# Where the last two copies of attention weights stand among ScalarE's work

## The chip, the core and the metric

The kernel runs on one core of a Trainium2 chip. The core has five engines with a queue each: TensorE (PE in the profile, with its weight loads as PEld), VectorE (DVE), ScalarE (ACT), GpSimd (POOL) and SyncE (SP, which here issues all DMAs). They run side by side and wait for each other by semaphores. The metric is the time of one execution on the device in microseconds (us); less is better. A profile is one further execution, recorded by the hardware profiler, with a time of its own.

## What is computed

Attention in which each query keeps only its 32 largest scores, followed by a two-layer network over all tokens. Batch 8, 8 heads, 576 positions, 64 per head, so 4608 tokens of 512 values; the hidden layer has 2048.

```python
scores = scale * np.matmul(q, k.transpose(0, 1, 3, 2))
kth = np.partition(scores, -top_k, axis=-1)[..., -top_k:-top_k + 1]
scores = np.where(scores >= kth, scores, -1000000000.0)
attn = np.exp(scores - np.max(scores, axis=-1, keepdims=True))
attn = attn / (np.sum(attn, axis=-1, keepdims=True) + 1e-09)
x = np.matmul(attn, v)          # then heads side by side: (4608, 512)
h = x @ w_in
g = np.where(h >= 1, h, np.where(h <= -1, 0.0, (h + 1) ** 2 / 4))
out = g @ w_out
```

All of it is in float32.

## The kernel before

**Steps.** The attention is cut into 144 steps (`n = 144`, `m` from 0 to 143). A step takes 128 queries of two heads. VectorE finds the 32nd largest score of each query, ScalarE takes the exponential, VectorE masks it (L467) and sums it. Four steps fill one chunk of 128 tokens; a chunk then goes through the network. There are 36 chunks, and the last is filled by the steps 140 to 143.

**From weights to values.** When step `m` begins, `divide` of step `m - 1` is issued: VectorE's reciprocal (L413), and on GpSimd the scaling of both heads' weights (L420) and a small subtraction into `excess` (L423). For step 143 there is no following step, so its `divide` comes in its own last slot. The weights must then be transposed for TensorE. In all but the first steps this goes by DMA: `move_w` (L493) has ScalarE split the float32 words into two halves of 16 bits (L497, two copies, one for each head, into the tile `halves`), writes them to DRAM (`rows<-halves`, L499), and puts the transposing read (`wT<-rows`, recorded at L296) on a list. The list `reads_of_rows` is issued by L832, in slot 0 of a step, and from step 141 on in every slot. `halves` has one buffer, `rows` three, `wT` four. `values` (L506) multiplies `wT` with the values (L514) into a PSUM buffer `po`, which ScalarE copies to `xT` (L527).

**The network.** `hidden(x)` is one piece of the first layer: sixteen matmuls (L547) for 256 of the 2048 hidden values of a chunk, so pieces 0 to 7. ScalarE reads a piece twice from PSUM, into `r` (L558) and `g` (L566), here called its reading. GpSimd then bounds, squares and adds (L573, L575, L576). `r` has two buffers: the reading of piece x waits until GpSimd is through with piece x - 2. `final(f)` is a matmul of the second layer (L586). Pieces and `po` share three PSUM buffers. The last chunk works in pieces of 128 and in half rows of the output (L561 to L563, L600, L612), with VectorE in GpSimd's place.

**Order.** The kernel writes out the order on each engine by hand (`tc.manual_schedule`). Each step has 7 slots. In each slot the top-k work goes first, then the transposes, then the copies of the weights, then the values, and last `advance` takes network work from the list `pending` up to an allowance. The closing steps 144 and 145 have no top-k work. Around the end, ScalarE's order is this. Step 143: reading 2 (slot 0), reading 3 (slot 1), reading 4 (slot 2), copy of step 142's weights (slot 3), reading 5 (slot 5). Step 144: `xT` copies of steps 140 and 141 (slot 2), copy of step 143's weights (slot 3). Step 145: readings 6 and 7, `xT` copies of 142 and 143, then the last chunk. TensorE in the same stretch: pieces 1 to 4, finals 0 and 1, piece 5, finals 2 and 3, values 140 and 141, piece 6, finals 4 and 5, piece 7, finals 6 to 9, values 142 and 143, the transpose `pworst`, finals 10 and 11, and then the last chunk's pieces between the remaining finals. GpSimd: piece 0, scaling and `excess` of 142, pieces 1 to 4, scaling and `excess` of 143, pieces 5 to 7.

The lines that place a copy:

```python
if slot == 3 and 1 <= m <= n and state[m - 1] is not None and not state[m - 1]["by_tensor"]:
    move_w(state[m - 1])
    ready_at[m - 1] = done[m - 1] + 15.0
```

`ready_at` is an estimate for the planner; its value for a step doesn't depend on the slot.

Of the kernel before, what the change touches and what calls it, by code (L numbers as in the profile page):

```python
# [26 lines left out]
def kernel(  # L27
# [99 lines left out]
    def load(pool, i, bufs=3, parts=1):  # L127
        if i < n_pieces * parts and i not in loaded:
            if room:
                loaded[i] = room[i % len(room)]  # L130
            else:
                loaded[i] = pool.tile([P, 2 * WC // parts], U32, name="raw", bufs=min(bufs, 2))
            c = i % parts * (WC // parts)
            nc.sync.dma_start(out=loaded[i], in_=pieces_of_weights[i // parts][1][:, c:c + WC // parts].bitcast(U32))
# [42 lines left out]
    def run(ctx, paired):  # L177
# [116 lines left out]
        def issue(x):  # L294
            while x:
                x.pop(0)()  # L296
# [179 lines left out]
        def transpose_w(st):  # L476
            w = st["e"]
            st["wT"] = wT = (late or words).tile([P, BLOCKS, P], F32, name="wT", bufs=4 if late else 1)
            pt = ps.tile([P, 2, NT, P], F32, name="pw", tag="a", bufs=2)
            for i in range(2):  # L480
                for c in range(NT):
                    nc.tensor.matmul(pt[:, i, c, :], w[:, i, main(i)][:, c * P:(c + 1) * P], st["rz"][:, i, :],  # L482
                                     start=True, stop=True)
            for i in range(2):
                nc.scalar.copy(wT[:, i * (NT + 1):i * (NT + 1) + NT], pt[:, i])
            pt = ps.tile([P, P], F32, name="pwt", tag="a", bufs=2)
            for i in range(2):
                nc.tensor.matmul(pt[i * TL:(i + 1) * TL, :], w[:, i, tail(i)], st["rz"][:, i, :], start=True, stop=True)
            nc.scalar.copy(wT[:, NT], pt)
# [3 lines left out]
        def move_w(st):  # L493
            st["wT"] = wT = late.tile([P, BLOCKS, P], F32, name="wT", bufs=4)
            halves = late.tile([P, 2, 2 * S], U16, name="halves")
            for i in range(2):
                nc.scalar.copy(halves[:, :, i * S:(i + 1) * S], st["e"][:, i, :].bitcast(U16).rearrange("p (k t) -> p t k", t=2))  # L497
            rows = dram.tile([P, 2, 2 * S], U16, name="rows")
            nc.sync.dma_start(out=rows, in_=halves)  # L499
            reads_of_rows.append(partial(nc.sync.dma_start_transpose, wT.bitcast(U16), rows.rearrange("p t k -> (p t) k")))  # L500
# [149 lines left out]
        n = len(steps)  # L650
# [18 lines left out]
        def convert(time):  # L669

            nonlocal converted, begun
            while begun < min(converted + (2 if paired else 1), n_pieces):
                pipe.append(convert_piece(words, begun, not paired))
                next(pipe[-1])
                begun += 1
            next(pipe.popleft())
            converted += 1
            usable[converted] = time
            for i in range(begun, converted + (len(room) or 2)):
                load(words, i)  # L680

        def inspect():
            nonlocal inspected
            if paired and inspected < 2 * n_pieces:
                inspect_piece(late, inspected)
                inspected += 1
# [54 lines left out]
        state = []  # L741
# [50 lines left out]
        def values_until(m):  # L792
            nonlocal valued, pe_time
            while valued < min(m, n):
                pe_time = max(pe_time, ready_at[valued]) + 1.25
                values(state[valued])
                state[valued] = None
                if valued in ready:
                    ch = ready[valued]
                    mlp(xTs[ch], rows_of(*chunks[ch]), mlp_pool, ch == len(chunks) - 1)  # L800
                valued += 1

        first_late = None
        for m in range(n + 2):
# [22 lines left out]
            for slot in range(SLOTS):  # L827
                now = start + (dve_time - start) * (slot + 1) / SLOTS
                for _ in range(parts[slot]):
                    next(top_k, None)  # L830
                if slot == 0 or m >= n - 3:
                    issue(reads_of_rows)  # L832
                if m < n and converted < n_pieces:
                    if slot in now_converting:
                        convert(now)
                elif slot == 3 and late is not None:
                    if m % 2:
                        inspect()
                if slot == 1 and 1 <= m <= n and state[m - 1]["by_tensor"]:
                    pe_time = max(pe_time, done[m - 1] + 2.0) + 1.0  # L840
                    transpose_w(state[m - 1])
                    ready_at[m - 1] = pe_time + 1.8
                if slot == 3 and 1 <= m <= n and state[m - 1] is not None and not state[m - 1]["by_tensor"]:
                    move_w(state[m - 1])
                    ready_at[m - 1] = done[m - 1] + 15.0
                if slot == 1 and late is not None and paired and m % 2 == 0:
                    load(late, inspected, 1, 2)
                if slot == 3:
                    issue(turns)
                    issue(loads)  # L850
                if slot == SLOTS - 1 and m == n + 1 and paired:
                    judge(ps, att)
                if slot == 2 and (early or m == first_late):
                    values_until(m)
                if slot == 2 and m >= n:
                    while pending and not pending[0][3] and (m > n or len(pending) > 24) and take():
                        pass
                    for _ in range(2 if m > n else 0):
                        take()
                    values_until(n if m > n else n - 2)  # L860
                if m == 0 and slot in (1, 2):
                    next(first)
                holding = not early and m % 2 == 0 and slot in (1, 2) and m < n
                if slot == 2 and not early:
                    if m % 2 == 0:
                        while len(reads) < 3 and pending and taken is not None and taken.__name__ == "hidden" and take():
                            pass
                    begin_until(min(m + 2, len(state)))
                    holding = False
                    issue_reads()  # L870
                    if m < n - 1:
                        values_until((m - 2) // 2 * 2)
                    begin_until(m + 3 - m % 2)
                if slot == 4 and early:
                    begin_at(m + 2)
                if slot == (6 if early else 1):
                    queries(m + (3 if early else 5))
                    if (m < n and prep is None and next_keys < B and steps[m][0] == next_keys - 1 and steps[m][1] >= 1
                            and (next_keys > 1 or converted == n_pieces)):
                        prep = (turned_keys_of if next_keys > 1 else keys_of)(next_keys)  # L880
                    if prep is not None and (m % 2 == 0 or next_keys == 1):
                        got = next(prep, None)
                        pe_time += 0.5 if next_keys < 2 else 0.0
                        if got is None:
                            prep, next_keys = None, next_keys + 1
                        else:
                            keys[next_keys] = got
                            value_loads = got.get("loads", value_loads)
                    elif value_loads is not None:
                        loads.append(partial(next, value_loads, None))  # L890
                if paired and early and spent == 0 and not pending:
                    rest = ps.tile([P, NT, P], F32, name="rest", tag="py", bufs=1)
                    for i in range(5):
                        nc.tensor.transpose(rest[:, i % NT, :], ident, ident)
                advance((EARLY_SHARE if early else share) / SLOTS if m < n - 2 else 32.0, now)
                slots_done += 1
                while bounds and (early or m >= n or bounds[0][0] < slots_done - 2):
                    bounds.popleft()[1]()
# [54 lines left out]
```

## Time and profile before

| | us |
|---|---|
| median of 3 runs | 1471.42 |
| lowest and highest run | 1471.32, 1472.72 |
| the profiled execution, its own time | 1469.45 |
| its span, first to last instruction | 1467.6 |
| busy VectorE, in the whole span | 1396.8 |
| busy ScalarE | 1161.1 |
| busy GpSimd | 928.5 |
| the 136 DMAs `rows<-halves`, issue to landing: shortest, median, longest | 2.8, 3.2, 5.2 |
| one L497 copy, median | 1.146 |

The times inside the profile count from the span's start. A line of the timeline gives the start, the length, the engine, the line in the code, the operation and its tiles; "x2" are two instructions in a row told as one. "SPq" is a DMA being issued on SyncE's queue. The chain of waits is followed back from the last instruction to what released each. The mean granted clock of TensorE over the span is 0.99 of full speed. Matmuls in float32 are recorded as two instructions each.

### The profile page before, as it was taken

Reading aid. Unit: us, or ns where it says so; the run is one execution under the profiler, and the core shown is the slowest. Engines: PE = TensorE matmul, PEld = TensorE weight load, DVE = VectorE, ACT = ScalarE, POOL = GpSimd, SP = SyncE. Lnnn points to the kernel's source line nnn. Section 1 sums busy time; section 2 is a strip of 40 time slices with the busy share of each in tenths; the row PEclk is TensorE's granted clock in tenths of the full one; section 3 lists DMA queues with packets and bytes.
Section 4 is the critical chain, followed back from the end, with each engine's and each line's share of the span. In section 5 each row is a group of like instructions: output and inputs, shape, how many; then the busy total and the mean of one; then the engine's idle time right before and its main releaser. Section 6 shows DMA issues by size and latency. Waiting matters only on the chain.

```text
span 1467.6 us, 31975 instructions
## 1 busy us (share of the span) xinstructions
PE 1430.7 (97%) x10731; PEld 1045.9 (71%) x10731; DVE 1396.8 (95%) x4392; ACT 1161.1 (79%) x2216; POOL 928.5 (63%) x1314
## 2 busy tenths in 40 slices
PE   7998899999999999999999999999999999999998
PEld 5766577777777777777777777777777777777677
DVE  6989999999999999999999999999999999999932
ACT  6986878888778888887778887888778888777643
POOL 3473576667666666666666666666666666676640
PEclk7999999999999999999999999999999999999999
DMA  7642767886668886987667986887668886665430
GB/s 240 194 133 64 189 180 196 218 206 172 173 171 212 217 206 178 221 216 178 167 172 201 216 213 173 219 225 184 159 168 199 218 212 175 171 172 153 137 105 18
DMA packets 517919, 264.87 MB, mean 180 GB/s; under 512 B 467696, under 2 KB 476144, under 8 KB 517744
## 3 DMA queue, kind: packets, MB, share of 16 engines
q1 hardware_dynamic: 517744, 262.73, 68.3%
q8 instruction: 87, 1.43, 0.4%
q14 instruction: 88, 0.72, 0.2%
HBM read 62.39 MB, written 104.86 MB: 114 GB/s over the span
## 4 chain that ended last, share of the span: by engine, by line
PE 78%; DVE 14%; ACT 4%; DMA 2%; issue 2%; SPq 0%; ACTq 0%
PE ph L547 29%; PE py L586 27%; PE sp L367 9%; PE po L514 8%; DVE more L388 3%; DVE e L467 3%; DVE more L381 1%; DVE less L381 1%; DVE tops L429 1%; DVE tops L437 1%; PE pw L482 1%; DVE tops L448 1%; DVE seconds L455 1%; PE po L522 1%; PE py_half L600 1%
## 5 line engine op out<-in xcount | busy, mean ns | idle before, releaser
L547 PEld LDWEIGHTS ph<-xT,w_in 128*128 128x128 f32 x4608 | 547.7, 192 | 97.8 <-issue 66.4
L547 PE MATMUL ph<-xT,w_in 128*128 128x128 f32 x4608 | 556.3, 276 | 2.7 <-ACT g L566 2.1
L586 PE MATMUL py<-w_out,g 128*128 128x512 f32 x1120 | 527.0, 598 | 2.0 <-ACT y L589 2.0
L573 POOL TENSOR_SCALAR r<-r 128x256 f32<-128x256 f32 x280 | 136.2, 487 | 398.2 <-ACT r L558 394.0
L388 DVE MATCH_REPLACE8 more<-tops,more 128x288 f32<-128x288 f32 x864 | 374.7, 437 | 0.0
L420 POOL TENSOR_SCALAR e<-e,rz 128x576 f32<-128x576 f32 x272 | 307.7, 1141 | 11.9 <-DVE rz L413 11.9
L586 PEld LDWEIGHTS py<-w_out,g 128*128 128x128 f32 x1120 | 194.2, 191 | 166.0 <-issue 164.7
L497 ACT COPY halves<-e 128x1152 uint16<-128x1152 uint16 x272 | 297.8, 1142 | 2.0 <-DMA rows<-halves 2.0
L576 POOL TENSOR_TENSOR g<-r,g 128x256 f32<-128x256 f32 x280 | 229.8, 821 | 22.0
L467 DVE SCALAR_TENSOR_TENSOR e<-s,kth,e 128x577 f32<-128x577 f32 x288 | 241.0, 872 | 0.1
L404 ACT ACTIVATE e<-s,nmax 128x576 f32<-128x576 f32 x288 | 222.5, 773 | 4.7
L558 ACT ACTIVATE r<-ph,half 128x256 f32<-128x256 f32 (+1 forms) x296 | 136.6, 462 | 99.5 <-PE ph L547 88.3
L368 ACT ACTIVATE s<-sp 128x576 f32<-128x576 f32 x288 | 171.9, 650 | 37.3 <-PE sp L367 34.6
L575 POOL TENSOR_TENSOR r<-r 128x256 f32<-128x256 f32 x276 | 180.2, 653 | 23.0
L367 PE MATMUL sp<-kT,qT 64*128 64x288 f32 x1024 | 163.1, 436 | 4.8 <-ACT kT L265 3.4
L514 PE MATMUL po<-wT,v_in 128*64 128x128 f32 x2048 | 139.1, 277 | 6.5 <-DMA wT<-rows 6.2
L367 PEld LDWEIGHTS sp<-kT,qT 64*128 64x128 f32 x1024 | 90.3, 189 | 76.2 <-issue 30.8
L381 DVE TENSOR_TENSOR more<-s 128x576 f32<-128x576 f32 x144 | 136.1, 945 | 7.9 <-ACT s L368 7.9
L514 PEld LDWEIGHTS po<-wT,v_in 128*64 128x64 f32 x2048 | 113.9, 137 | 31.7 <-issue 13.0
L566 ACT ACTIVATE g<-ph,minus 128x256 f32<-128x256 f32 x280 | 130.8, 467 | 0.0
L429 DVE MAX8 tops<-more 128x8 f32<-128x288 f32 x288 | 125.3, 442 | 0.0
L401 DVE MAX8 tops<-more 128x8 f32<-128x288 f32 x288 | 116.2, 442 | 0.0
(95 smaller groups left out, 1340.8 us busy)
## 6 DMA issues: line engine op xcount, KB each, us to landing
rows<-halves SPq DMA_DIRECT2D x136, 576.0 KB, 3.2
lines<-parts SPq DMA_DIRECT2D x52, 256.0 KB, 3.4
q_in<-in_q_dram SPq DMA_DIRECT2D x32, 256.0 KB, 4.0
v_in<-in_v_dram SPq DMA_DIRECT2D x32, 256.0 KB, 3.9
raw<-in_moe_w_in_dram SPq DMA_DIRECT2D x32, 256.0 KB, 3.4
raw<-in_moe_w_out_dram SPq DMA_DIRECT2D x32, 256.0 KB, 3.4
out_dram<-y SPq DMA_DIRECT2D x31, 256.0 KB, 3.3
kT<-in_moe_w_in_dram SPq DMA_DIRECT2D x8, 512.0 KB, 4.8
```

The source lines that it names most:

```text
L367: nc.tensor.matmul(*x, start=True, stop=True)
L368: nc.scalar.activation(s[:, :, c0:c1], sp[:, :, 0:SH], AF.Copy, scale=SCALE)
L388: nc.vector.match_replace(out=st["rest"][:, i, :], in_to_replace=eight(st["tops"], i, r - 8), in_values=src[:, i, :], imm_value=LOWEST)
L404: nc.scalar.activation(e[:, i, :], s[:, i, :], AF.Exp, bias=nmax[:, i:i + 1])
L420: nc.gpsimd.tensor_scalar(st["e"][:, i, :], st["e"][:, i, :], rz[:, i:i + 1], 1.0, ALU.mult, ALU.mult)
L467: nc.vector.scalar_tensor_tensor(out=st["all"][1][:, i, :], in0=st["all"][0][:, i, :], scalar=last[i], in1=st["all"][1][:, i, :], op0=ALU. ...
L497: nc.scalar.copy(halves[:, :, i * S:(i + 1) * S], st["e"][:, i, :].bitcast(U16).rearrange("p (k t) -> p t k", t=2))
L514: nc.tensor.matmul(po[j * D:(j + 1) * D], v_in[:, h, c, :] if c < NT else tail_values(v_tl, h, t), wT[:, block(j, c)], start=(c == 0), sto ...
L547: nc.tensor.matmul(ph[:, i], w_in[:, kk, f * P:(f + 1) * P], xT[:, kk], start=(kk == 0), stop=(kk == NK - 1))
L575: nc.gpsimd.tensor_tensor(out=r, in0=r, in1=r, op=ALU.mult)
L576: nc.gpsimd.tensor_tensor(out=g, in0=r, in1=g, op=ALU.add)
L586: nc.tensor.matmul(py[0], gs[f // group][:, f % group], w_out[:, f, :], start=(f == 0), stop=(f == NF - 1))
```

## The change

One condition is changed. Up to step 142 the copy of the preceding step's weights stays in slot 3. In step 143 (`m = n - 1`) it stands in slot 1, in step 144 (`m = n`) in slot 0. With it moves what `move_w` issues: the two ScalarE copies, the DMA `rows<-halves`, and, one slot later, the DMA `wT<-rows`. Nothing else changes place.

```diff
-                if slot == 3 and 1 <= m <= n and state[m - 1] is not None and not state[m - 1]["by_tensor"]:
+                if slot == (3 if m < n - 1 else n - m) and 1 <= m <= n and state[m - 1] is not None and not state[m - 1]["by_tensor"]:
                     move_w(state[m - 1])
                     ready_at[m - 1] = done[m - 1] + 15.0
```

## The prediction

> **What bounds the kernel now.** I read the page's busy times first, then the chain of waits near the end, then the timeline of that stretch, and last the clock by windows. Steps are counted by `m`: 144 steps (0 to 143) and two closing ones, 144 and 145. "Copy 142" is the pair of L497 copies that `move_w` makes of the weights of step 142; "rows 142" and "transpose 142" are its two DMAs, "values 142" its L514 matmuls.
>
> ```profile
> PE 1430.7 (97%) x10731; PEld 1045.9 (71%) x10731; DVE 1396.8 (95%) x4392; ACT 1161.1 (79%) x2216; POOL 928.5 (63%) x1314
> ```
>
> TensorE is busy for 97% of the span, so a change in the order of ScalarE's work pays only where TensorE waits. The change touches the steps 143 and 144, so I asked the chain of waits for that stretch (start, length, what):
>
> ```profile
> 1410.45 2.33 PE po L514 x40
> ...
> 1418.27 2.74 PE py L586 x7
> 1421.02 4.69 DMA wT<-rows
> 1425.71 0.14 issue
> 1425.84 2.40 PE po L514 x20
> 1428.24 0.30 PE pworst L915
> 1428.54 2.15 PE py L586 x4
> 1430.70 0.89 PE ph L547 x8
> ```
>
> The chain is TensorE alone until 1421.02, and TensorE alone again from 1425.84 to the last output. Between them stands one transfer, transpose 143. TensorE itself works until 1422.95 (values 142 runs under the transfer) and then waits until 1425.84: 2.89 us. Then 20 matmuls of L514 take 2.40 us, where 40 took 2.33 us at 1410: TensorE runs at half speed after the wait. The timelines of ScalarE, GpSimd and SyncE show what made the transfer late (start, length, what, and in brackets the idle time before it and what ended it):
>
> ```profile
> 1406.40 0.48 ACT L558 ACTIVATE r<-ph,half 128x256 f32<-128x256 f32 x1 [3.42 <-POOL g L576]
> ...
> 1409.00 2.20 ACT L497 COPY halves<-e 128x1152 uint16<-128x1152 uint16 x2
> ...
> 1415.14 2.21 ACT L497 COPY halves<-e 128x1152 uint16<-128x1152 uint16 x2 [2.04 <-DMA rows<-halves]
> ```
>
> ```profile
> 1411.96 1.48 POOL L420 TENSOR_SCALAR e<-e,rz 128x576 f32<-128x576 f32 x2
> 1413.40 0.20 POOL L423 TENSOR_TENSOR excess<-seconds,kth 128x2 f32<-128x2 f32 x1
> ```
>
> ```profile
> 1411.22 0.33 SPq L499 DMA_DIRECT2D rows<-halves  x1
> 1415.10 2.48 SPq L296 DMA_TRANSPOSE wT<-rows  x1
> 1417.67 0.53 SPq L499 DMA_DIRECT2D rows<-halves  x1
> 1421.02 2.70 SPq L296 DMA_TRANSPOSE wT<-rows  x1
> ```
>
> Copy 142 runs at 1409.00, though its weights were scaled by 1403.6 (GpSimd's L420 at 1402.08 and L423 ended 1403.71). It stood behind two readings of the hidden layer (L558 and L566), and these behind GpSimd. Copy 143 has its data by 1413.60, but `halves` is a single buffer, and rows 142 has still to be read out of it: 2.04 us of waiting. Then rows 143 stands 0.3 us behind the issue of transpose 142 in SyncE's queue, and lands in 3.35 us beside that transfer. The clock, by windows (columns: length, then busy us of PE, PEld, DVE, ACT, POOL, granted clock, DMA share, GB/s):
>
> ```profile
> 1423.00:1424.00 1.00, 0.00 (x0) 0.00 (x0) 0.00 (x0) 0.27 (x1) 0.00 (x0) 1.00 1.19 214
> 1426.00:1427.00 1.00, 1.00 (x12) 1.00 (x13) 0.00 (x0) 0.00 (x0) 0.00 (x0) 0.50 0.00 0
> 1428.00:1429.00 1.00, 1.00 (x5) 0.51 (x3) 0.39 (x2) 0.27 (x1) 0.00 (x0) 0.50 0.00 0
> 1429.00:1430.00 1.00, 1.00 (x3) 0.43 (x2) 0.06 (x1) 0.00 (x0) 0.00 (x0) 0.85 0.00 0
> ```
>
> Half clock lasts from about 1425.9 to 1429.3, some 3.4 us, and costs half of it, 1.7 us.
>
> **What the Trainium skill says.** "TensorE: Matmul & The Clock Gate", table under "Why this matters for your kernels", asks for no idle gaps above about 3 us, or TensorE falls to half clock. The trace agrees in kind, with a lower limit: a gap of 2.11 us at 139.4 is followed by a clock of 0.50, and so is this one of 2.89 us; gaps of 1.25 us at 148.8, 1.28 us at 193.9 and 2.07 us at 93.8 are not. The same page, Part 1 ("Engine queue depths"), has ScalarE as strictly first in, first out: a copy that is placed ahead of readings runs ahead of them, and holds them up while it waits. The trace shows this order throughout. "DMA: Bandwidth & Descriptors", "Two DMAs through the same engine are not ordered", has a reader of a DMA's data wait for that DMA's completion. Here each transpose is issued when its rows have landed (1411.22 to 1415.10, 1417.67 to 1421.02), so every microsecond of landing passes on.
>
> **The change part by part.** No instruction is added or removed. In step 143 copy 142 goes from slot 3 to slot 1, and in step 144 copy 143 from slot 3 to slot 0. Each takes its `rows` DMA with it, and its transpose, issued at the start of the next slot. What they pass on ScalarE: copy 142 passes the readings of hidden pieces 3 and 4 (ScalarE at 1406.40 and 1408.27); copy 143 passes the two `xT` copies of values 140 and 141 (L527, 1411.82 and 1412.84). On SyncE they pass nothing: the order there stays output, rows 142, transpose 142, rows 143, transpose 143. GpSimd's and TensorE's queues are as before.
>
> Copy 142: ScalarE is free at 1402.98, and GpSimd has scaled both heads and written `excess` by 1403.71. The copy runs from 1403.75 to 1405.95 (2.20). The next reading waited for GpSimd's release of `r` until 1406.40 anyway, so the move costs ScalarE nothing; the cover is 0.45 us, and with less of it that reading would be late by the difference, with GpSimd busy until 1408.20 before it needs it. SyncE had issued the output's DMA at 1403.87 for 0.57 us and is free. Rows 142 goes at 1405.97 and lands after 2.84 us (the three before it, at 1379.11, 1387.30 and 1398.59, took 2.84, 2.83 and 2.84) at 1408.81; transpose 142 is issued until 1411.3. Values 142 needs it at 1421.6: no effect.
>
> Readings 3 and 4 stay where GpSimd lets them. Reading 5 no longer waits for copy 142 (to 1411.20) but for GpSimd's release at 1410.11 (its L576 of 1409.38 and 0.73 us). GpSimd doesn't gain: it is busy without a break from 1402.08 to 1415.46, so scaling 143 stays at 1411.96 to 1413.44 and `excess` at 1413.60.
>
> Copy 143: `halves` is free since 1408.81, ScalarE since about 1411.0. What is late next is GpSimd. The trace has no copy that waits for the scaling, so whether it may start on one head's scaling, or only after the whole group with `excess`, isn't shown. Bounds: 1412.75 with both copies back to back (end 1415.0), or 1413.64 after `excess` (end 1415.84). I take the second: the three stand together in GpSimd's queue, and it is the careful value. Rows 143 goes at 1415.86, with the queue free and no transfer beside it: 2.84 us, so 1418.70. Transpose 143 to the first matmul of values 143: 4.69 + 0.14 = 4.83 us as now, so 1423.5. TensorE is through with values 142 at 1422.95 as before: it waits 0.6 us instead of 2.89. So 2.3 us go, and after 0.6 us the clock shouldn't fall: another 1.7 us. The sum is 4.0 us. With the early bound the wait is gone: 2.89 + 1.7 = 4.6 us.
>
> What the `xT` copies pay: they run at 1415.9 to 1416.4 instead of 1411.8 and 1412.8. The PSUM buffer of values 140 is wanted again by hidden piece 7, whose matmuls start at 1416.49. The first copy frees it at 1416.15: 0.3 us to spare. Even a stall there would not add up, since TensorE then needs 6.5 us to values 143, and transpose 143 arrives 7.7 us after copy 143 ends: the transfer still ends last. Readings 6 and 7 come 0.8 us sooner than now (1417.25).
>
> From 1430.70 on the chain is TensorE's own and moves as one. The profiled execution would take 1469.45 - 4.0 = 1465.4 us (span 1463.6). The runs' median lies 1.97 us above that execution; with the same difference I forecast 1467.4 us, 0.27% less.
>
> **The rivals.**
> - No wait left (early bound): 1466.8. For it: the scaling of the first head ends 0.9 us ahead of `excess`. Against: it needs a signal between the two scalings of one step.
> - The landing is late again or the clock falls all the same: 2.3 us are gained, or with a landing of 3.88 us 1.2 us plus the clock's 1.7. That gives 1468.5 to 1469.1. For it: rows 142 took 3.88 us with no other large transfer beside it, and that can strike rows 143. Against: three in a row took 2.84.
> - That landing of 3.88 belongs to the profiled execution only. Then copy 143 starts at 1414.1 in ordinary runs, rows 143 at 1416.6 behind transpose 142, lands at 1420.0, and values 143 starts at 1424.8 after 1.85 us of idling, perhaps at full clock. The change gains 1.3 us: 1470.1. Against: the ordinary runs are not shorter than the profiled one.
> - Slower: copy 143 at the head of ScalarE's queue, waiting for GpSimd, holds the `xT` copies, the PSUM buffer and the readings behind it. Its price is each microsecond by which the copy ends after 1418.15, where values 143 would start at 1425.84 again. That takes GpSimd's scaling 2.3 us later than now. Were the scaling to stand behind three more hidden pieces of 1.87 us (1408.20 to 1410.07), it came 5.6 us later, values 143 3.3 us later than today: 1474.7. For it: GpSimd is the fullest queue here and the copy now waits for it directly. Against: nothing in GpSimd's queue moves.
>
> **How the numbers follow.** A measurement here can tell about 0.2% (2.9 us) from no change. Chances: forecast 0.54, no wait left 0.16, late landing or low clock 0.12, gain only 1.3 us 0.12, slower 0.06. Faster by over 0.2%: the first two and a third of the next, 0.74; within 0.2%: 0.20; slower 0.06. The range goes from 1466.2 (no wait left, and 0.6 for the runs' spread, under half of the 1.4 us between the three shown) to 1469.8, which takes in the late landing.
>
> **What would show it.** In the changed profile: copy 142 at about 1403.8, ahead of the reading at 1406.4; copy 143 with a wait for GpSimd instead of one for rows; 2.84 us for rows 143; an idle gap under 1 us ahead of the last L514 group, 20 matmuls there in about 1.2 us, and a clock of 1.00. It would be wrong if copy 143 waited past 1415, if hidden piece 7 waited for L527, or if the gap stayed above 2 us.

## The result and the profile after

| | before | changed |
|---|---|---|
| median of the runs, us | 1471.16 | 1466.73 |
| ratio, 95% interval | | 0.9968 (0.9960 to 0.9977) |
| the profiled execution, us | 1469.45 | 1466.98 |
| its span, us | 1467.6 | 1465.2 |

The change takes about 4.7 us off (0.32%; the interval gives 3.4 to 5.9). One of the changed kernel's 22 runs took 2430.53 us at a granted clock of 0.56 and is left out of the ratio; the median of the other 21 is 1466.48, 4.68 us under that of before. The forecast was 1467.4. In the page of the changed kernel TensorE is busy for 98% of the span:

```profile
PE 1428.9 (98%) x10731; PEld 1045.9 (71%) x10731; DVE 1400.4 (96%) x4392; ACT 1160.6 (79%) x2216; POOL 930.1 (63%) x1314
```

In the chain of waits of the changed kernel (start, length, what) the stretch in question has no transfer in it any more:

```profile
1411.79 2.33 PE po L514 x40
...
1419.61 3.44 PE py L586 x8
1423.04 2.33 PE po L514 x40
1425.38 0.20 PE pworst L915
1425.58 1.72 PE py L586 x4
1427.30 0.89 PE ph L547 x8
```

Values 142 and 143 are now one piece of 40 matmuls in 2.33 us. Before, values 143 alone took 2.40 us after a wait of 2.89. The windows of the changed kernel show the clock there (length, then busy us of PE, PEld, DVE, ACT, POOL, granted clock, DMA share, GB/s):

```profile
1423.00:1424.00 1.00, 1.00 (x19) 1.00 (x20) 0.00 (x0) 0.00 (x0) 0.00 (x0) 1.00 0.17 35
1424.00:1425.00 1.00, 1.00 (x24) 1.00 (x22) 0.00 (x0) 0.27 (x1) 0.00 (x0) 1.00 0.00 0
1425.00:1426.00 1.00, 1.00 (x11) 0.59 (x8) 0.35 (x2) 0.27 (x1) 0.00 (x0) 1.00 0.00 0
```

The clock stays at full speed (1.00). How the copies came to be in time is told by the timelines of ScalarE, GpSimd and SyncE of the changed kernel:

```profile
1404.20 2.21 ACT L497 COPY halves<-e 128x1152 uint16<-128x1152 uint16 x2 [0.27 <-POOL e L420]
1407.34 0.47 ACT L558 ACTIVATE r<-ph,half 128x256 f32<-128x256 f32 x1 [0.94 <-POOL g L576]
...
1414.18 2.20 ACT L497 COPY halves<-e 128x1152 uint16<-128x1152 uint16 x2 [1.75 <-POOL e L420]
1416.29 0.43 ACT L527 COPY xT<-po 128x128 f32<-128x128 f32 x2
```

```profile
1413.40 1.47 POOL L420 TENSOR_SCALAR e<-e,rz 128x576 f32<-128x576 f32 x2
1414.83 0.20 POOL L423 TENSOR_TENSOR excess<-seconds,kth 128x2 f32<-128x2 f32 x1
```

```profile
1406.43 0.33 SPq L499 DMA_DIRECT2D rows<-halves  x1
1409.62 2.45 SPq L296 DMA_TRANSPOSE wT<-rows  x1
1416.41 0.34 SPq L499 DMA_DIRECT2D rows<-halves  x1
1419.24 2.37 SPq L296 DMA_TRANSPOSE wT<-rows  x1
```

The wait for rows is gone; both copies wait for GpSimd's scaling instead. Copy 143 begins when the first head is scaled (1413.40 and 0.74 us for one of the two), not after `excess`.

To compare executions that reach the end a little earlier or later, I measure one stretch in each profile: from the first L514 matmul of values 140 to the first L547 matmul of the last chunk. The timeline of TensorE has these two lines for it before:

```profile
1410.38 1.09 PE L514 MATMUL po<-wT,v_in 128*64 128x128 f32 x16
...
1430.53 1.05 PE L547 MATMUL ph<-xT,w_in 128*128 128x128 f32 x8
```

and these in the changed kernel:

```profile
1411.72 1.09 PE L514 MATMUL po<-wT,v_in 128*64 128x128 f32 x16
...
1427.13 1.05 PE L547 MATMUL ph<-xT,w_in 128*128 128x128 f32 x8
```

It is 1430.53 - 1410.38 = 20.15 us before and 1427.13 - 1411.72 = 15.41 us in the changed kernel: 4.74 us less. The two spans differ by 2.4 us only. The changed kernel's profile reaches the stretch 1.34 us later, and 1.33 us of that is there already where the run of hidden pieces ahead of it begins (1399.42 in the chain against 1398.09), before copy 142. It also ends 1.0 us later after its last output was issued (5.87 us against 4.87). Neither belongs to the change; the medians given above, 4.68 us apart, agree with the stretch.

| kernel | stretch, us | ratio to before, 95% interval |
|---|---|---|
| before | 20.15 | 1 |
| changed | 15.41 | 0.9968 (0.9960 to 0.9977) |
| e1, only copy 142 moved | 15.57 | 0.9967 (0.9955 to 0.9978) |
| e2, only copy 143 moved | 19.09 | 0.9992 (0.9982 to 1.0002) |
| e3, a second buffer | 20.33 | 0.9998 (0.9990 to 1.0007) |
| e4, TensorE kept busy | 18.68 | 0.9989 (0.9980 to 0.9998) |
| e5, scaling 2.2 us late | 17.64 | 0.9972 (0.9963 to 0.9980) |
| e6, scaling 4.4 us late | 20.38 | 0.9988 (0.9980 to 0.9997) |
| e7, slot 1 in every step | | 1.1277 (1.1261 to 1.1292) |
| e8, the tile of e5 and e6 alone | 15.41 | 0.9961 (0.9946 to 0.9975) |
| e9, the changed kernel again | 15.42 | 0.9968 (0.9959 to 0.9978) |

### The profile page after: what moved, and what is told of

Its sections match the earlier page's. It is cut to its first block, busy times and chain, and to the rows that moved or that the text cites. A ratio compares the mean times of both kernels' runs of the same rounds, so it can differ in the third digit from the quotient of the medians.

```text
span 1465.2 us, 31976 instructions
## 1 busy us (share of the span) xinstructions
PE 1428.9 (98%) x10731; PEld 1045.9 (71%) x10731; DVE 1400.4 (96%) x4392; ACT 1160.6 (79%) x2216; POOL 930.1 (63%) x1314
## 4 chain that ended last, share of the span: by engine, by line
PE 87%; DVE 6%; ACT 3%; DMA 2%; issue 1%; SPq 1%; ACTq 0%; DVEq 0%
PE ph L547 33%; PE py L586 31%; PE sp L367 10%; PE po L514 10%; PE po L522 1%; DVE more L388 1%; DVE e L467 1%; DMA wT<-rows 1%; PE py_half L600 1%; ACT s L368 1%; DVE more L381 1%; ACT halves L497 1%; PE pw L482 1%; DVE bits L156 1%; DVE tops L429 0%
## 5 line engine op out<-in xcount | busy, mean ns | idle before, releaser
L547 PEld LDWEIGHTS ph<-xT,w_in 128*128 128x128 f32 x4608 | 548.7, 193 | 98.0 <-issue 64.9
L547 PE MATMUL ph<-xT,w_in 128*128 128x128 f32 x4608 | 557.2, 277 | 2.9 <-ACT g L566 1.9
L573 POOL TENSOR_SCALAR r<-r 128x256 f32<-128x256 f32 x280 | 148.5, 530 | 393.2 <-ACT r L558 389.9
L497 ACT COPY halves<-e 128x1152 uint16<-128x1152 uint16 x272 | 297.8, 1142 | 2.0 <-POOL e L420 2.0
L420 POOL TENSOR_SCALAR e<-e,rz 128x576 f32<-128x576 f32 x272 | 289.5, 1074 | 12.6 <-DVE rz L413 12.6
L576 POOL TENSOR_TENSOR g<-r,g 128x256 f32<-128x256 f32 x280 | 226.4, 808 | 22.0
L368 ACT ACTIVATE s<-sp 128x576 f32<-128x576 f32 x288 | 171.6, 649 | 46.7 <-PE sp L367 45.1
L575 POOL TENSOR_TENSOR r<-r 128x256 f32<-128x256 f32 x276 | 183.5, 665 | 23.0
L367 PE MATMUL sp<-kT,qT 64*128 64x288 f32 x1024 | 161.7, 433 | 5.3 <-ACT kT L265 3.9
L367 PEld LDWEIGHTS sp<-kT,qT 64*128 64x128 f32 x1024 | 89.9, 188 | 75.9 <-issue 30.6
L514 PE MATMUL po<-wT,v_in 128*64 128x128 f32 x2048 | 139.0, 277 | 3.7 <-DMA wT<-rows 3.4
L381 DVE TENSOR_TENSOR more<-s 128x576 f32<-128x576 f32 x144 | 133.0, 924 | 6.1 <-ACT s L368 6.1
L514 PEld LDWEIGHTS po<-wT,v_in 128*64 128x64 f32 x2048 | 113.8, 137 | 28.8 <-issue 15.4
```

The costliest lines, as they stand in the source:

```text
L367: nc.tensor.matmul(*x, start=True, stop=True)
L368: nc.scalar.activation(s[:, :, c0:c1], sp[:, :, 0:SH], AF.Copy, scale=SCALE)
L420: nc.gpsimd.tensor_scalar(st["e"][:, i, :], st["e"][:, i, :], rz[:, i:i + 1], 1.0, ALU.mult, ALU.mult)
L514: nc.tensor.matmul(po[j * D:(j + 1) * D], v_in[:, h, c, :] if c < NT else tail_values(v_tl, h, t), wT[:, block(j, c)], start=(c == 0), sto ...
L547: nc.tensor.matmul(ph[:, i], w_in[:, kk, f * P:(f + 1) * P], xT[:, kk], start=(kk == 0), stop=(kk == NK - 1))
L575: nc.gpsimd.tensor_tensor(out=r, in0=r, in1=r, op=ALU.mult)
```

## The experiments

**Which of the two moves carries the gain.** The first kernel moves copy 142 alone, the second copy 143 alone.

```diff
-if slot == 3 and 1 <= m <= n and ...
+if slot == (1 if m == n - 1 else 3) and 1 <= m <= n and ...
```

> Copy 142 in slot 1 of step 143, copy 143 left in slot 3 of step 144. Theory (the early copy 142 frees the buffer and SyncE's queue, and the move of copy 143 adds next to nothing): copy 143 starts behind the two xT copies, about 0.3 us later than in the changed kernel, TensorE still waits under 0.5 us before the last L514 group and keeps its full clock: 4.4 us less than before, as in the whole change. Rival (copy 143 must itself go ahead of the xT copies): at most half of the gain, 2 us or less.

```diff
-if slot == 3 and 1 <= m <= n and ...
+if slot == (0 if m == n else 3) and 1 <= m <= n and ...
```

> Copy 143 in slot 0 of step 144, copy 142 left in slot 3 of step 143. Theory: copy 143 now waits at the head of ScalarE's queue for rows 142, so it starts no earlier than before; the xT copies behind it are late, hidden piece 7 stalls about 1 us, but values 143 starts when it did: within 1 us of before. Rival (the move of copy 143 carries the gain): 2.3 to 4.7 us less.

Copy 142 alone brings the whole gain: a stretch of 15.57 us and a ratio that can't be told from the changed kernel's. Copy 143 ran at 1415.10 there, behind both `xT` copies, where it had no idle time ahead of it, and values 142 and 143 still follow each other without a wait that the timeline of TensorE would show:

```profile
1423.74 1.09 PE L514 MATMUL po<-wT,v_in 128*64 128x128 f32 x16
...
1424.98 1.09 PE L514 MATMUL po<-wT,v_in 128*64 128x128 f32 x16
```

Copy 143 alone brings 1.06 us of the stretch, and in the runs no change that can be told. The timeline of TensorE of the kernel that moves copy 143 alone shows why the stretch is shorter all the same:

```profile
1416.38 1.88 PE L586 MATMUL py<-w_out,g 128*128 128x512 f32 x4
1419.85 2.05 PE L547 MATMUL ph<-xT,w_in 128*128 128x128 f32 x16 [1.59 <-ACT xT L527]
...
1428.17 1.09 PE L514 MATMUL po<-wT,v_in 128*64 128x128 f32 x16 [1.59 <-DMA wT<-rows]
```

The timeline of ScalarE has the copy:

```profile
1417.43 2.21 ACT L497 COPY halves<-e 128x1152 uint16<-128x1152 uint16 x2 [3.61 <-POOL g L576]
```

Copy 143 waits at the head of ScalarE's queue for 3.61 us. The bracket names GpSimd, but the copy starts within 0.04 us of the issue of transpose 142 (1417.39), which waits for rows 142 to land. So I read its wait as one for rows 142, as was expected. It holds the `xT` copies, so hidden piece 7 waits for its PSUM buffer: the stall that the prediction named. TensorE idles 1.59 us there and 1.59 us at values 143, in all 0.3 us more than the 2.89 of before. But neither of them is followed by the half clock: 0.3 us more of waiting stand against 1.7 us of clock saved. The stretch is shorter by 1.06 us, not by 1.4: a stretch with two idle times grows by some 0.5 us more than they last (3.68 us over the changed kernel's for 3.18 here; 2.23 for 1.74 in e5 below).

**The buffer or the queue.** Copy 143 gets a buffer of its own, a `kT` tile that is no longer read by then.

```diff
-            halves = late.tile([P, 2, 2 * S], U16, name="halves")
+            if st["m"] == n - 1:
+                halves = stage.tile([P, NHP, S], F32, name="kT").rearrange("p h n -> p (h n)").bitcast(U16)
+                halves = halves[:, 0:4 * S].rearrange("p (t x) -> p t x", t=2)
+            else:
+                halves = late.tile([P, 2, 2 * S], U16, name="halves")
```

> The order of before, but copy 143 writes into a buffer of its own, so it doesn't wait for rows 142. Theory (SyncE's queue is the next thing late: rows 143 stands behind the issue of transpose 142): copy 143 starts 1 to 2 us sooner, rows 143 is issued when it was, gain 0 to 0.5 us. Rival (the single buffer alone makes the wait): 2.3 us less or more.

The timelines of ScalarE and SyncE of this kernel (L501 is the copy, now into the `kT` tile):

```profile
1411.84 2.21 ACT L501 COPY kT<-e 128x1152 uint16<-128x1152 uint16 x2
```

```profile
1410.19 0.33 SPq L503 DMA_DIRECT2D rows<-halves  x1
1414.32 2.50 SPq L296 DMA_TRANSPOSE wT<-rows  x1
1416.91 0.54 SPq L503 DMA_DIRECT2D rows<-kT  x1
1420.24 2.47 SPq L296 DMA_TRANSPOSE wT<-rows  x1
```

The copy no longer waits and ends at 1414.05. Its rows are issued at 1416.91 all the same, 2.86 us later: SyncE first waits for rows 142 to land, then issues transpose 142 for 2.50 us. The time doesn't move. So the wait for the buffer was not what held the end; rows 142 was, by two ways at once, and an earlier copy 142 opens both.

**How much of the gain is clock.** In the order of before, TensorE gets work during the wait.

```diff
                 values(state[valued])
+                if paired and valued == n - 2:
+                    busy = ps.tile([P, NT, P], F32, name="busy", tag="a", bufs=2)
+                    for i in range(12):
+                        nc.tensor.matmul(busy[:, i % NT, :], ident, ident, start=True, stop=True)
```

> The order of before, with 12 matmuls of the identity that nobody reads, between values 142 and values 143 on TensorE (2.7 us of work in a wait of 2.9). Theory: values 143 starts when it did, but at full clock: 1.7 us less than before. If the long wait stands in the profiled execution only (1.85 us in ordinary runs): 0 to 0.9 us more than before. If the half clock comes from something else than the idle time, no gain.

The timeline of TensorE of this kernel:

```profile
1420.37 2.94 PE L800 MATMUL busy<-ident 128*128 128x128 f32 x24
1423.48 1.09 PE L514 MATMUL po<-wT,v_in 128*64 128x128 f32 x16 [0.17 <-DMA wT<-rows]
1424.37 0.42 PE L514 MATMUL po<-wT,v_tail 128*64 128x128 f32 x4
```

The 12 matmuls are recorded as 24. Values 143 still comes with the transfer, but sixteen recorded matmuls take 1.09 us instead of 1.98. The stretch is 1.47 us shorter and the runs 0.11% (1.6 us; the interval gives 0.3 to 2.9). The half clock is a cost of its own, and it comes from the idle time. This run and the two before it also settle the rival that the late landing of rows 142 belonged to one execution: it took 4.28, 4.13 and 3.87 us in them, after 3.88 in the kernel before.

**How much room is left, and what a later scaling costs.** The changed kernel with more work on GpSimd ahead of the scaling of step 143, on a tile that nothing else uses: three operations in e5, six in e6, none in e8. The two lines that make the tile and fill it at the start are left out here.

```diff
             else:
+                for i in range(3 if paired and st["m"] == n - 1 else 0):
+                    nc.gpsimd.tensor_scalar(idle, idle, 1.0, 1.0, ALU.mult, ALU.mult)
                 for i in range(2):
                     nc.gpsimd.tensor_scalar(st["e"][:, i, :], st["e"][:, i, :], rz[:, i:i + 1], 1.0, ALU.mult, ALU.mult)
```

> The changed kernel, with three more GpSimd operations of 0.74 us (on a tile nobody reads) ahead of the scaling of step 143: 2.2 us later. Theory (after the change the copy waits for GpSimd alone, with 0.3 us to spare at values 143): TensorE idles 1.9 us in two places, about 1.1 us at hidden piece 7 behind the late xT copy and 0.8 us at values 143, too short for the half clock: 1.9 us more than the changed kernel, so 2.5 us less than before. If the half clock comes all the same: 3.6 us more than the changed kernel. If GpSimd has slack: no change against it.

> The same with six operations: 4.5 us later. Theory: TensorE idles 3.3 us at hidden piece 7 and 0.9 us at values 143, and the first idle costs a half clock of 1.7 us: 5.9 us more than the changed kernel, 1.4 us more than before. Without the half clock 4.2 us more than the changed kernel.

> The changed kernel with the extra tile of the two late-scaling kernels, but none of their operations. If the tile (other addresses behind it) is free: 4.4 to 4.7 us less than before, as the changed kernel. If it is what made the two late kernels some 1.5 us faster than their stretch at the end explains: about 6 us less than before.

The timeline of TensorE of the kernel with the scaling 2.2 us late (L551 is a hidden piece, L518 the values):

```profile
1418.57 2.05 PE L551 MATMUL ph<-xT,w_in 128*128 128x128 f32 x16 [0.90 <-ACT xT L531]
...
1426.13 1.09 PE L518 MATMUL po<-wT,v_in 128*64 128x128 f32 x16 [0.84 <-DMA wT<-rows]
```

The same timeline with the scaling 4.4 us late:

```profile
1418.72 2.76 PE L551 MATMUL ph<-xT,w_in 128*128 128x128 f32 x16 [3.03 <-ACT xT L531]
1421.28 4.60 PE L590 MATMUL py<-w_out,g 128*128 128x512 f32 x8
```

With 2.2 us the idle time is 0.90 and 0.84 us where 1.1 and 0.8 were expected, the clock stays up, and the stretch grows by 2.23 us. With 4.4 us TensorE idles 3.03 us ahead of hidden piece 7, and the clock falls to half 1.2 us after the piece has begun (at 1419.88): the next eight matmuls of the second layer (L590) take 4.60 us instead of 3.60. The stretch grows by 4.97 us where 5.9 were expected, because TensorE, slowed down, reaches values 143 after the transfer, so that the second idle time is gone. Against the runs of before, both kernels are faster than their stretches say: 4.1 us where the stretch gives 2.5, and 1.8 us where it gives a loss of 0.2. The tile alone doesn't settle that: its ratio of 0.9961 (5.7 us less) lies between what was expected of a tile that costs nothing and of one that explains it, and its interval takes in both. Why the two are faster stays open.

**Why not everywhere.** The kernel before, with slot 1 for every step.

```diff
-if slot == 3 and 1 <= m <= n and ...
+if slot == 1 and 1 <= m <= n and ...
```

> The kernel before, with the copy in slot 1 in every step. Theory: copies 142 and 143 gain 4 us at the end as in the change; in the other steps copies wait at the head of ScalarE's queue for GpSimd's scaling, in front of exponentials and readings, and TensorE is late for it by up to a few tenths of a us per step: between 4 us less and 30 us more than before; over 4 us less only if the steps before also gain.

The waits of this kernel over the whole span (what waited for what: us in total, times, longest):

```profile
ACT halves L497 <- POOL e L420: 303.9, 113, 3.4
PEld sp L367 <- ACT s L368: 171.5, 124, 4.3
DVE more L381 <- ACT s L368: 162.6, 67, 3.6
```

It is 12.8% slower, 188 us, far outside what was expected. In the kernel before no copy waits for the scaling (ScalarE idles 2.0 us ahead of L497 in the whole span, for rows), and VectorE waits 7.9 us for L368 at L381. Here, 113 times a copy waits at the head of ScalarE's queue for the scaling, for 2.7 us on average. Behind them stand the readings of the next scores (L368), and without these VectorE can't start its top-k work (162.6 us of waiting) and TensorE can't reuse the scores' PSUM (L367). This is the slower rival's mechanism, at work in steps where it has something behind it to hold up. The clock is lower too: its mean is 0.963 against 0.990, so over the spans some 61 us of full clock were withheld against some 14 before, an estimate. How much of the 188 us that is was not tried. In the last two steps no scores are left to read: the last L368 begins at 1376.8 in the changed kernel.

**The changed kernel again.**

> The changed kernel once more, on the same chip and beside the same runs of before as the one with the extra tile: 4.4 to 4.7 us less than before, and the stretch from values 140 to the last chunk's first piece 15.4 us long again.

The ratio is 0.9968 once more, and the stretch 15.42 us.

## Why the prediction was right

- What bounds the end: right. One transfer stood in TensorE's chain, its wait of 2.89 us is gone, and 20 matmuls of values 143 no longer run at half speed. "DMA: Bandwidth & Descriptors" of the Trainium skill ("Two DMAs through the same engine are not ordered") has a DMA that reads another's data issued only when that one is complete. The traces agree: of the 136 transposes `wT<-rows` in each of the eleven profiles, none was issued before its rows had landed.
- Copy 142 moves at no cost: right. It ran at 1404.20, and reading 3 behind it then still waited 0.94 us for GpSimd (a cover of 0.45 us had been worked out). Rows 142 took 3.19 us there, not the 2.84 that had been taken over from the steps before; nothing waited for it. TensorE's chain is unbroken up to values 142.
- "What is late next is GpSimd": right, both copies wait for L420. The value that was taken for the start of copy 143, after `excess`, was the wrong one of the two bounds. It starts 0.04 us after the first head's scaling. In this execution `excess` ended at 1415.03, so the copy came 0.85 us sooner than by the value taken. The forecast's residual wait of 0.6 us was therefore none. So it is the rival "no wait left" that came true, to which the prediction gave a chance of 0.16, and its 1466.8 lies nearer to the result than the forecast's 1467.4. The sum had 4.0 us for one and 4.6 for the other; the stretch lost 4.74.
- Rows 143 in 2.84 us with a free queue: right, 1416.41 to 1419.24 is 2.83.
- The clock's share of 1.7 us: right in the profiled execution. The kernel with the busy TensorE gives 1.47 us in the stretch. The 3.27 us that it still lies above the changed kernel's are the wait: in that execution 3.11 us from the start of the idle matmuls to values 143. But the prediction took the length of a gap for what decides (2.11 us yes, 2.07 us no), and that was wrong: where the gap lies counts too, as the last section shows.
- The `xT` copies: they ran at 1416.29, and piece 7 started at 1417.66 without a wait. The reserve was some 1.1 us, where 0.3 had been worked out, since the copy came sooner. That a stall there doesn't add up held in e2 and e5, where the idle time was divided between the two places. It failed in e6, where the half clock after the first stall made TensorE the later one.
- The price of the slower rival, 1 us for each microsecond that copy 143 ends after 1418.15: in e6 it ended at 1418.50, in an execution that reaches the stretch 0.79 us sooner than before's, so 1.14 us past the point. Its stretch is 0.23 us longer than before's, so the price was too high.
- The forecast treated both moves as parts of the gain. The runs show that the move of copy 142 is enough, and that the move of copy 143 alone gains nothing that the runs can tell.

## What to carry to other kernels

When a late transfer ends a stage, follow it back past the first wait to the one that feeds it: here the buffer's wait and the queue's wait both hung on the copy one step earlier, and a second buffer alone moved nothing. A copy can go ahead of other work in an engine's queue where that work waits for something else anyway; the same move cost 188 us where the queue behind it fed the busiest engines. Price an idle TensorE with the half clock that can follow: filling the wait with idle matmuls already gave back a third of the gain.

## What the hardware showed

The length of an idle time doesn't decide alone on the half clock. In the kernel e2, 2.07 us of idle time (first line, timeline of TensorE) were followed by a clock of 0.50 (second line, windows, third number from the end):

```profile
96.15 1.23 PE L482 MATMUL pw<-diag,e 128*128 128x128 f32 x4 [2.07 <-ACT diag L417]
96.00:97.00 1.00, 0.85 (x4) 0.85 (x5) 1.00 (x3) 1.00 (x3) 1.00 (x1) 0.50 0.45 106
```

The same idle time near 94 us (2.06 or 2.07 us) left the clock at full speed in nine of the eleven profiles. And in e3 one of 3.32 us left it at 1.00:

```profile
160.94 1.09 PE L518 MATMUL po<-wT,v_in 128*64 128x128 f32 x16 [3.32 <-DMA wT<-rows]
156.00:164.00 8.00, 4.68 (x57) 3.48 (x54) 8.00 (x28) 7.46 (x16) 3.12 (x5) 1.00 0.65 166
```

What the falls of the clock to 0.50 have in common is a grid in time; the traces list when the granted clock changes. Between 60 and 1460 us, in each of the eleven profiles, all falls begin a whole number of 3.413 us apart. In the kernel before they begin at 142.47, 162.95 and 1425.88 us, 6 and 370 such steps from one to the next. If the time is cut into slices at these steps, the idle time within one slice tells which of them end in a fall: all 47 slices with over 1.9 us of it, 7 of the 17 with 1.7 to 1.9 us, and none of the other 4432.

In e2 a step came near the end of the 2.07 us, at 96.00, and 1.92 us of them lay in one slice. In e3 a step at 159.50 cut the 3.32 us into 1.88 and 1.44. In the kernel before, the whole 2.89 us lay in the slice that ends at 1425.88. Each of the two idle times of 1.59 us in e2 is too short for a fall wherever it lies. So the 1.7 us of clock are shown for the profiled execution only. By an estimate from these numbers, a wait of 2.89 us is cut into two parts that are both too short (under 1.7 to 1.9 us) in one execution out of four to seven.

The page "TensorE: Matmul & The Clock Gate" of the Trainium skill ("Why this matters for your kernels") puts the limit at about 3 us. Here 1.83 us were enough in one place (e9, at 140.43, fall at 143.64), and 3.32 us were not in another.

Rows 142, in its old place, took 3.87 to 4.28 us to land in the four kernels that leave it there, where the three before it in the kernel before took 2.83 or 2.84. In its new place it took 3.11 to 3.57 in six kernels (3.19 in the changed one). Why the old place is slower was not tried.
